# Causal mask of gated linear attention: a triangle multiplied on VectorE as PSUM is read, in place of ScalarE copies and a GpSimd selection

## The chip, the core and the metric

The kernel runs on one core of a Trainium2 chip, in one launch. The metric is device microseconds of that core; the time before is the median of three runs. A profiled execution of its own gives the rows below.

## What is computed

Three stages, one after the other, all in float32:

```python
# 1: gated linear attention, B, H, S, D = 4, 8, 768, 48
f = 1.0 / (1.0 + np.exp(-f_logit))
for t in range(S):
    state = f[:, :, t, :, None] * state + np.einsum('bhd,bhe->bhde', k[:, :, t], v[:, :, t])
    y[:, :, t] = np.einsum('bhd,bhde->bhe', q[:, :, t], state)
# 2: causal softmax attention with E = 4 experts, two chosen for each token; d_model 384, Hd 64
logits = x @ w_gate            # topk, w from these
scores = scale * (x @ wq[e]) @ (x @ wk[e]).T   # causal, softmax -> a
out += mask[..., None] * w[:, :, kk:kk + 1] * (a @ (x @ wv[e]) @ wo[e])
# 3: rotation and mixing over tokens and channels
theta = x @ w_theta
u = x + w_tok_r @ (x * np.cos(theta)) + w_tok_i @ (x * np.sin(theta))
result = u + np.maximum(u @ w_ch, 0.0)
```

## The kernel before

Sequence positions are cut into chunks of 128, so there are six chunks for each of four batches, 24 in all. Within a chunk the gated recurrence becomes dense products. `gate` and `cum` make the running sums of the log gates (a scan on VectorE, line 270) and scale k and q by their exponentials (lines 280 and 281). `att` multiplies k by q for eight heads into two PSUM banks of 128x512 (line 302). Only products of an earlier key with a later query may stay, so `att` then copies each bank to the tile `g_a` on ScalarE (line 90, through `copy`) and clears the other half with a selection on GpSimd (line 309), which cannot start before its copy is done. `out` multiplies the masked `g_a` by v (line 319) and adds what the state carries over (line 325); `state` updates the state (lines 341 to 354). There is one buffer of `g_a`.

`turn_x` splits the result into a rounded part `m_xs`, `m_x` and a remainder for the matmuls of stage 2. There, `val` and `qk` project (lines 477 and 518), and 96 units of one expert and one block of 128 queries go through `score` (558 and 560), `top` (row maxima on VectorE, 566), `exp` (ScalarE, 580), `turn` (transposes 619, copied to `m_aT`), `av` (639), `sum` (651 to 656) and `mix` (668), whose two banks are copied or reduced to `m_xt` and stored.

On the side, 30 blocks of weights that arrive as doubles are turned to float32 with four VectorE operations and one of ScalarE each (lines 107 to 112): three of `w_theta`, and 27 that are stored to a DRAM tile `w_dram` from one staging buffer `w_f`. Stage 3 (`Moe2`, lines 765 to 791) starts when stage 2 is through; its first rotations are made ahead.

All PSUM results share eight banks called `M`. Every piece above is put into one list, `plan`, with a time worked out from the numbers in the table `TUNE`, and the list is walked in order of time. The framework's scheduler then sets each engine's queue, which runs in order. Keys that begin with `e_` say which engine makes a copy, 1 for VectorE and 0 for ScalarE.

Of the kernel before, what the change touches and what calls it, by code (L numbers as in the profile page):

```python
# [7 lines left out]
F32 = mybir.dt.float32  # L8
# [5 lines left out]
OP = mybir.AluOpType  # L14
# [5 lines left out]
P = 128  # L20
# [4 lines left out]
NP = H // 2  # L25
# [30 lines left out]
def make_consts(nc, pool):  # L56
    k = Bag()
    nc.scalar.preload_act_table_set("natural_log_exp_and_others")
    k.ones = pool.tile([P, P], BF16, name="c_ones")
    nc.vector.memset(k.ones, 1.0)  # L60
    k.ident = pool.tile([P, P], F32, name="c_ident")
    ii = k.ident.bitcast(I32)
    nc.gpsimd.iota(ii, pattern=[[1, P]], base=0, channel_multiplier=-1)
    k.one = pool.tile([P, 1], F32, name="c_one")
    nc.vector.memset(k.one, 1.0)
    k.negmask = pool.tile([P, P], BF16, name="c_negmask")
    nc.vector.tensor_scalar(k.negmask, ii, 0.0, NEG, op0=OP.is_gt, op1=OP.mult)
    nc.vector.tensor_scalar(k.ident, ii, 0.0, None, op0=OP.is_equal)
    k.identb = pool.tile([P, P], BF16, name="c_identb")
    nc.vector.tensor_copy(k.identb, k.ident)  # L70
    k.least = pool.tile([P, 2, E, E], F32, name="c_least")
    nc.gpsimd.memset(k.least, TINY)
    nc.gpsimd.affine_select(k.least, k.least, pattern=[[0, 2], [-1, E], [1, E]], base=0, channel_multiplier=0,
                            compare_op=OP.is_ge, fill=0.0)
    k.magic = pool.tile([P, 1], F32, name="c_magic")
    nc.vector.memset(k.magic, MAGIC)
    k.hpi = pool.tile([P, 1], F32, name="c_hpi")
    nc.vector.memset(k.hpi, TWO_PI / 4)
    return k
# [9 lines left out]
def copy(nc, what, out, in_):  # L89
    (nc.vector.tensor_copy if TUNE["e_" + what] else nc.scalar.copy)(out, in_)  # L90
# [141 lines left out]
class Gla:  # L232
# [63 lines left out]
    def att(self, b, c):  # L296
        nc, t = self.nc, self.T[b, c]
        banks = [self.pM.tile([P, NP, P], F32, name="M") for _ in range(2)]
        for hp in range(NP):
            for j, ps in enumerate(banks):  # L300
                r = slice(64 * j, 64 * j + D)
                nc.tensor.matmul(ps[:, hp, :], t.k[r, hp, :], t.q[r, hp, :], start=True, stop=True)  # L302
        yield
        a = self.wk.tile([P, 2, NP, P], F32, name="g_a")
        for j, ps in enumerate(banks):
            copy(nc, f"a{j}", a[:, j], ps)
        yield
        for part in ([a[:, j] for j in range(2)] if b * NT + c < 2 or TUNE['e_mask'] else [a.rearrange("p j n t -> p (j n) t")]):
            nc.gpsimd.affine_select(part, part, pattern=[[0, part.shape[1]], [1, P]], base=0, channel_multiplier=-1,  # L309
                                    compare_op=OP.is_ge, fill=0.0)  # L310
        t.a = a

    def out(self, b, c):
        nc, t = self.nc, self.T[b, c]
# [399 lines left out]
class Moe2:  # L714
# [123 lines left out]


TUNE = dict(  # L840
    y_cum0=0, y_tr0=1.375, y_att0=0.126, y_att1=0.78, y_state0=0, y_turn_x0=0, y_val0=1.729, y_qk0=3.02,
    y_turn0=1.114, y_sum0=0.96, y_sum1=0, y_mix0=1.233, dF1=-0.745, dF2=0.116, dF3=0.979, nw0=44, nw1=9, nw2=10,
    w1=-16.404, w2=-7.547, late_rot=543.893, w_pre=8.523, d_top=0, d_exp=1.229, d_turn=0.792, d_av=0.944,
    d_sum=1.962, alpha=1.291, pre=7.133, l_mix=4.433, mix_sp=14.358, lo0=-10.454, lo_sp=0.19, f0=-21.897,
    f1=-10.255, f2=-0.315, f3=7.902, f4=18.093, f5=44.165, F=46.18, sp=27.869, l_gate=6.566, l_cum=3.387,
    l_tr=7.532, l_att=5.306, l_out=2.063, l_state=2.008, l_xt=0.38, l_val=7.067, v0=7.7, v1=9.035, vsp=5.54,
    l_qk=5.413, qk_sp=0.359, l_q1=10.13, l_top2=2.06, tok0=1.418, tok1=411.066, late0=404.775, late1=504.708,
    late_gap=3.057, ewv=-18.203, ewq=-36.87, esp=3.509, l_factor=4.261, y_factor0=2.51, tok_p=0.109, y_gate0=0.594,
    e_mask=1, e_kn=0, e_a0=0, e_a1=0, e_v=0, e_q=1, e_k=0, e_t0=0, e_t1=0, e_t2=0, e_t3=1, e_yh=0, e_mix0=1,
    e_mix1=0, e_x=0, e_x3=0, e_f=0, y_factor1=0,  # L850
)


# [117 lines left out]
def kernel(ctx: ExitStack, tc: tile.TileContext, arg, out: bass.AP):  # L971
# [10 lines left out]
    rows.tok = (wd[:S], wd[S:2 * S]) if arg.w_tok[0].dtype == I64 else arg.w_tok  # L982
    rows.ch = wd[2 * S:, :DM] if arg.w_ch.dtype == I64 else arg.w_ch
    c = make_consts(nc, const)

    def body(fast):
# [79 lines left out]
```

## Time and profile before

| what | value |
|---|---|
| median of three runs | 647.75 us (647.14 to 649.93) |
| the profiled execution's own time | 653.63 us |
| span of its instructions | 651.7 us |
| mean granted TensorE clock | 0.968 |
| busy: TensorE, VectorE, ScalarE, GpSimd | 604.5, 387.6, 363.6, 131.4 us |

The span runs from the first to the last instruction; the profiled execution's own time has 1.9 us more around it. A busy TensorE is not one at its peak, since the ends of pipelined matmuls are modelled.

### The profile page before, as it was taken

How to read it: one execution, taken by the hardware profiler on the slowest of the kernel's cores; microseconds unless marked ns; L12 is line 12 of the kernel's file. 1: busy time of each engine (PE TensorE's matmuls, PEld its weight loads, DVE VectorE, ACT ScalarE, POOL GpSimd, SP SyncE). 2: the span in 40 equal slices, each digit the busy share in tenths (PEclk: the TensorE clock that was granted, in tenths of full speed). 3: DMA queues.
4: the chain of work that ended last, by engine and by line, in shares of the span. 5: the costliest groups of instructions: out<-in, count | busy, mean ns of one | idle time of the engine just before them, and what ended most of it. 6: DMA issues, size and time to landing. Idle time of an engine off the chain costs nothing.

```text
span 651.7 us, 12652 instructions
## 1 busy us (share of the span) xinstructions
PE 604.5 (93%) x4613; PEld 527.8 (81%) x4613; DVE 387.6 (59%) x932; ACT 363.6 (56%) x919; POOL 131.4 (20%) x205
## 2 busy tenths in 40 slices
PE   5798998999978899999899999988999999999995
PEld 4677767777857778887778878768999999999995
DVE  6788887988888466465566354774775253232221
ACT  6666776765585665666664464876785282130000
POOL 5533211210212012111010010013663141130000
PEclk7699999998999799999899999999899999999999
DMA  7556555665556232324334000616623212000010
GB/s 266 177 173 193 165 182 170 186 191 161 177 187 202 101 98 81 94 83 127 94 96 121 29 32 32 234 57 223 202 78 117 61 49 73 25 24 22 28 49 29
DMA packets 46678, 76.42 MB, mean 117 GB/s; under 512 B 6672, under 2 KB 25616, under 8 KB 46608
## 3 DMA queue, kind: packets, MB, share of 16 engines
q1 hardware_dynamic: 46608, 75.53, 36.6%
q8 instruction: 38, 0.62, 0.4%
q14 instruction: 32, 0.26, 0.1%
HBM read 53.68 MB, written 19.46 MB: 112 GB/s over the span
## 4 chain that ended last, share of the span: by engine, by line
PE 61%; ACT 4%; DMA 4%; DVE 4%; POOL 1%; issue 1%; SPq 1%; ACTq 0%; DVEq 0%; POOLq 0%
PE M L765 22%; PE M L788 6%; PE M L518 5%; PE M L668 5%; PE M L639 4%; PE M L558 4%; PE M L619 3%; PE M L477 3%; PE M L319 2%; PE M L302 2%; PE M L325 2%; DMA g_f<-in_fT_dram 2%; DMA w_dram<-w_f 1%; PE M L777 1%; ACT m_a L580 1%
## 5 line engine op out<-in xcount | busy, mean ns | idle before, releaser
L580 ACT ACTIVATE m_a<-M,m_m 128x384 f32<-128x384 f32 (+4 forms) x128 | 69.2, 548 | 14.3 <-DVE m_m L566 7.1
L566 DVE TENSOR_REDUCE m_m<-M 128x1 f32<-128x384 f32 (+4 forms) x128 | 61.0, 499 | 10.6 <-PE M L560 8.8
L558 PE MATMUL M<-m_ks,m_qs 64*128 64x384 f32 (+4 forms) x256 | 56.0, 482 | 3.1 <-ACT m_aT L90 1.0
L619 PE MATMUL M<-c_ident,m_a 128*128 128x128 f32 x336 | 53.3, 280 | 3.5 <-ACT m_aT L90 1.3
L94 ACT CAST t_uh<-M 128x384 fp32r<-128x384 f32 x24 | 11.3, 474 | 79.3 <-PE M L777 79.3
L309 POOL TENSOR_SCALAR_AFFINE_SELECT g_a<-g_a 128x512 f32<-128x512 f32 x48 | 35.0, 749 | 94.5 <-ACT g_a L90 94.5
L90 ACT COPY m_aT<-M 128x384 f32<-128x384 f32 (+3 forms) x96 | 43.0, 450 | 16.4 <-PE M L619 16.1
L639 PE MATMUL M<-m_aT,m_v 128*64 128x256 f32 (+1 forms) x384 | 43.7, 359 | 0.0
L129 POOL TENSOR_TENSOR t_z0l<-t_ra,t_z0h 128x384 fp32r<-128x384 f32 x23 | 25.0, 1086 | 91.3 <-ACT t_z0h L128 82.9
L619 PEld LDWEIGHTS M<-c_ident,m_a 128*128 128x128 f32 x336 | 38.2, 143 | 5.7 <-ACT m_a L580 2.1
L270 DVE TENSOR_TENSOR_SCAN g_cum<-g_inside,g_f 128x512 f32<-128x512 f32 x24 | 30.6, 1273 | 15.2 <-ACT g_f L266 14.1
L639 PEld LDWEIGHTS M<-m_aT,m_v 128*64 128x64 f32 x384 | 28.7, 137 | 13.0 <-issue 2.1
L319 PE MATMUL M<-g_a,g_v 128*64 128x128 f32 x384 | 30.9, 286 | 7.9 <-POOL g_a L309 7.3
L95 DVE TENSOR_TENSOR t_ul<-M,t_uh 128x384 fp32r<-128x384 f32 x24 | 13.3, 556 | 41.2 <-ACT t_uh L94 41.2
L558 PEld LDWEIGHTS M<-m_ks,m_qs 64*128 64x128 f32 x256 | 24.4, 188 | 16.5 <-issue 4.5
L668 PE MATMUL M<-m_wh,m_yh 128*128 128x384 f32 x96 | 34.1, 357 | 3.7 <-ACT m_aT L90 3.1
L791 DVE SCALAR_TENSOR_TENSOR t_o<-M,t_u 128x384 f32<-128x384 f32 x24 | 13.4, 556 | 39.4 <-PE M L788 39.4
L354 POOL COPY g_block<-g_state 64x192 f32<-64x192 f32 x40 | 18.7, 469 | 86.3 <-DVE g_state L349 73.0
L319 PEld LDWEIGHTS M<-g_a,g_v 128*64 128x64 f32 x384 | 22.9, 140 | 14.1 <-POOL g_a L309 11.2
L302 PE MATMUL M<-g_q,g_k 48*128 48x128 f32 x384 | 32.9, 306 | 1.5 <-DVE g_q L281 0.9
L765 PE MATMUL M<-t_z0h,t_w 128*128 128x384 f32 x96 | 32.8, 342 | 0.0
L668 PE MATMUL M<-m_wh,m_yl 128*128 128x384 f32 x96 | 32.5, 338 | 0.3 <-DVE m_yl L656 0.3
(245 smaller groups left out, 1688.5 us busy)
## 6 DMA issues: line engine op xcount, KB each, us to landing
t_dram<-m_xt SPq DMA_DIRECT2D x24, 384.0 KB, 2.8
g_f<-in_fT_dram SPq DMA_DIRECT2D x24, 256.0 KB, 3.1
g_k<-in_kT_dram SPq DMA_DIRECT2D x24, 256.0 KB, 3.2
g_q<-in_qT_dram SPq DMA_DIRECT2D x24, 256.0 KB, 3.0
g_v<-in_vp_dram SPq DMA_DIRECT2D x24, 256.0 KB, 3.1
w_dram<-w_f SPq DMA_DIRECT2D x27, 192.0 KB, 3.1
w_d<-in_w_tok_r_dram SPq DMA_DIRECT2D x12, 384.0 KB, 3.4
w_d<-in_w_tok_i_dram SPq DMA_DIRECT2D x12, 384.0 KB, 3.9
```

The costliest lines, as they stand in the source:

```text
L90: (nc.vector.tensor_copy if TUNE["e_" + what] else nc.scalar.copy)(out, in_)
L302: nc.tensor.matmul(ps[:, hp, :], t.k[r, hp, :], t.q[r, hp, :], start=True, stop=True)
L309: nc.gpsimd.affine_select(part, part, pattern=[[0, part.shape[1]], [1, P]], base=0, channel_multiplier=-1, compare_op=OP.is_ge, fill=0.0)
L319: nc.tensor.matmul(y[64 * r:64 * r + 64, hp, :], t.v[:, 2 * hp + r, :], t.a[:, r, hp, :], start=hp == 0, stop=c == 0, skip_group_check=True)
L558: nc.tensor.matmul(ps, q[own, rows], k[own, cols], start=True, stop=cols.stop < W)
L566: nc.vector.tensor_reduce(m, ps, axis=AX.X, op=OP.max, negate=True)
L580: self.nc.scalar.activation(a[:, cols], ps, AF.Exp, bias=t.m, accum_out=st.den[:, c, i % 2, e % 2:e % 2 + 1])
L619: nc.tensor.transpose(ps[:, (j - j0) * P:(j - j0 + 1) * P], t.a[:, j * P:(j + 1) * P], self.k.ident)
L639: nc.tensor.matmul(y[64 * r:64 * r + 64, o:TQ], st.v[j][:, m * HD:(m + 1) * HD], st.aT[m][:, j, o:], start=j == 0, stop=True, skip_group_c ...
L668: nc.tensor.matmul(ps[:, :DM], st.y[pr, t // 2][a][:, o], self.wl[c][:, 2 * w0 + pr, :], start=n == 0, stop=n == 5)
L765: nc.tensor.matmul(ps, self.wT[c][h][s][:, (g * G + j) * P:(g * G + j + 1) * P], self.Z[b, s][c][l], start=s == 0 and n == 0, stop=s == NT ...
L788: nc.tensor.matmul(ps[:, :DM], uT[a][:, j, :], self.wl[c][:, j, :], start=n == 0, stop=n == 8)
```

## The change

`att` no longer copies and selects. One VectorE multiply for each bank reads the products out of PSUM, multiplies them by a triangle of ones and zeros (`c_upper`, made once at the start and read again for each of the four head pairs) and writes `g_a`. The second pause inside `att` and its third part go. Four copies change engines by the table: `val`'s `m_v` (`e_v`), the second bank of `mix` for batches 1 to 3 (`e_mix1`) and `turn_x`'s `m_x` (`e_x3`) go from ScalarE to VectorE, `qk`'s `m_qs` (`e_q`) goes from VectorE to ScalarE. `e_a1` and `e_mask` no longer have an effect. Most of the other numbers, which order the pieces, are a little different; TensorE gets 66 warm-up matmuls in place of 63 and otherwise the same matmuls.

```diff
+    k.upper = pool.tile([P, P], F32, name="c_upper")
+    nc.vector.tensor_scalar(k.upper, ii, 0.0, None, op0=OP.is_ge)
...
         yield
-        a = self.wk.tile([P, 2, NP, P], F32, name="g_a")
+        a = t.a = self.wk.tile([P, 2, NP, P], F32, name="g_a")
+        if TUNE["e_fm"]:
+            for j, ps in enumerate(banks):
+                nc.vector.tensor_tensor(a[:, j], ps, self.k.upper.rearrange("p (o t) -> p o t", o=1).to_broadcast([P, NP, P]), op=OP.mult)
+            return
         for j, ps in enumerate(banks):
             copy(nc, f"a{j}", a[:, j], ps)
         yield
         for part in ([a[:, j] for j in range(2)] if b * NT + c < 2 or TUNE['e_mask'] else [a.rearrange("p j n t -> p (j n) t")]):
             nc.gpsimd.affine_select(part, part, pattern=[[0, part.shape[1]], [1, P]], base=0, channel_multiplier=-1,
                                     compare_op=OP.is_ge, fill=0.0)
-        t.a = a
...
-    late_gap=3.057, ewv=-18.203, ewq=-36.87, esp=3.509, l_factor=4.261, y_factor0=2.51, tok_p=0.109, y_gate0=0.594,
-    e_mask=1, e_kn=0, e_a0=0, e_a1=0, e_v=0, e_q=1, e_k=0, e_t0=0, e_t1=0, e_t2=0, e_t3=1, e_yh=0, e_mix0=1,
-    e_mix1=0, e_x=0, e_x3=0, e_f=0, y_factor1=0,
+    ewv=-21.53, ewq=-33.37, esp=3.509, l_factor=4.203, y_factor0=1.518, tok_p=0.558, y_gate0=0.06, e_mask=1, e_fm=1,
+    e_kn=0, e_a0=0, e_a1=1, e_v=1, e_q=0, e_k=0, e_t0=0, e_t1=0, e_t2=0, e_t3=1, e_yh=0, e_mix0=1, e_mix1=1, e_x=0,
+    e_x3=1, e_f=0, y_factor1=0,
```

VectorE's queue at the first chunk, before: the scaled k and q of the second chunk, a remainder of the mixing weights, and what follows.

```order
L280 TENSOR_TENSOR g_k<-g_k,g_ei 128x512
L281 TENSOR_TENSOR g_q<-g_q,g_f 128x512
L95 TENSOR_TENSOR m_wl<-m_a,m_wh 128x384
L187 TENSOR_SCALAR m_ks<-m_ks 128x256
L270 SCALAR_TENSOR_TENSOR g_cum<-g_inside,g_f 128x512
L349 TENSOR_TENSOR g_state<-M,g_dec 128x192
```

The same place now:

```order
L282 TENSOR_TENSOR g_k<-g_k,g_ei 128x512
L283 TENSOR_TENSOR g_q<-g_q,g_f 128x512
L97 TENSOR_TENSOR m_wl<-m_a,m_wh 128x384
L309 TENSOR_TENSOR g_a<-M,c_upper 128x512 x2
L189 TENSOR_SCALAR m_ks<-m_ks 128x256
L354 TENSOR_TENSOR g_state<-M,g_dec 128x192
L272 SCALAR_TENSOR_TENSOR g_cum<-g_inside,g_f 128x512
```

The first chunk's two multiplies stand behind the second chunk's scaling, and the third chunk's scan has moved behind the first state.

VectorE's queue around the sixth gated output `m_ys`, before; `w_d`, `w_b` and `w_f` are the raw, half made and finished weights.

```order
L651 TENSOR_TENSOR m_ys<-M,m_f 128x256
L107 TENSOR_SCALAR w_b<-w_d 128x384
L108 SCALAR_TENSOR_TENSOR w_b<-w_d,w_b 128x384
L656 TENSOR_TENSOR m_yl<-m_ys,m_yh 128x256
L109 SCALAR_TENSOR_TENSOR w_b<-w_d,w_b 128x384
L566 TENSOR_REDUCE m_m<-M 128x1 x2
L112 SCALAR_TENSOR_TENSOR w_f<-w_g,w_b 128x384
```

The same place now:

```order
L656 TENSOR_TENSOR m_ys<-M,m_f 128x256
L661 TENSOR_TENSOR m_yl<-m_ys,m_yh 128x256
L571 TENSOR_REDUCE m_m<-M 128x1 x2
L114 SCALAR_TENSOR_TENSOR w_f<-w_g,w_b 128x384
L109 TENSOR_SCALAR w_b<-w_d 128x384
L110 SCALAR_TENSOR_TENSOR w_b<-w_d,w_b 128x384
L309 TENSOR_TENSOR g_a<-M,c_upper 128x512 x2
L92 COPY m_v<-M 128x260
L111 SCALAR_TENSOR_TENSOR w_b<-w_d,w_b 128x384
```

Two multiplies and a copy of `m_v` now stand inside a weight block's conversion. Over the whole queue, 27 stored blocks stood ahead of the tenth gated output before, and 24 do now; ahead of the first, 4 before and 2 now.

ScalarE's queue between the two exponentials of a pair of units, before:

```order
L580 ACTIVATE m_a,m_den_827<-M,m_m 128x256
L90 COPY g_a<-M 128x512 x2
L90 CAST m_xs<-M 128x3x128
L90 CAST m_x_912<-M 128x128
L580 ACTIVATE m_a,m_den_827<-M,m_m 128x256
```

The same pair now:

```order
L585 ACTIVATE m_a,m_den_822<-M,m_m 128x256
L92 COPY m_aT<-M 128x128
L585 ACTIVATE m_a,m_den_822<-M,m_m 128x256
```

The two copies of `g_a` and the cast of `m_x` are gone from between them, and the cast of `m_xs` stands elsewhere.

## Rows read from the trace of the kernel before

**Rows 1.** Windows by stage: length, busy of each engine (instructions), granted clock, DMA share, GB/s.

```profile
core 0: us, PE busy (x) PEld busy (x) DVE busy (x) ACT busy (x) POOL busy (x), PEclk, DMA share, GB/s
0.00:45.00 45.00, 33.39 (x273) 27.98 (x275) 32.18 (x52) 29.35 (x60) 21.36 (x38) 0.81 0.62 204
45.00:455.00 410.00, 381.19 (x3248) 311.56 (x3249) 278.57 (x748) 264.76 (x715) 65.15 (x125) 0.98 0.42 134
455.00:652.00 197.00, 189.88 (x1095) 188.28 (x1094) 76.89 (x134) 69.54 (x145) 44.91 (x42) 0.99 0.20 63
```

**Rows 2.** Chain that ended last, start of stage 3: start, length, what.

```profile
454.69 15.28 PE M L765 x73
```

**Rows 3.** Waits of PE, 0 to 455 us: total, times, longest.

```profile
PE M L518 <- ACT m_aT L90: 8.9, 4, 3.1
PE M L319 <- POOL g_a L309: 7.3, 10, 2.4
PE M L291 <- DVE g_k L280: 5.9, 2, 4.9
PE M L668 <- ACT m_aT L90: 3.1, 2, 1.6
...
PE M L619 <- ACT m_aT L90: 1.3, 2, 1.1
...
PE M L302 <- DVE g_q L281: 0.9, 1, 0.9
```

**Rows 4.** Timeline of one chunk's mask, 201 us: start, length, what, [idle before].

```profile
200.77 1.05 ACT L90 COPY g_a<-M 128x512 f32<-128x512 f32 x2
...
201.41 1.70 POOL L309 TENSOR_SCALAR_AFFINE_SELECT g_a<-g_a 128x512 f32<-128x512 f32 x2 [5.01 <-ACT g_a L90]
...
202.26 0.43 PE L319 MATMUL M<-g_a,g_v 128*64 128x128 f32 x2 [1.11 <-POOL g_a L309]
...
203.16 1.09 PE L319 MATMUL M<-g_a,g_v 128*64 128x128 f32 x14 [0.47 <-POOL g_a L309]
```

**Rows 5.** Groups of instructions that the change removes or moves.

```profile
L309 POOL TENSOR_SCALAR_AFFINE_SELECT g_a<-g_a 128x512 f32<-128x512 f32 x48 | 35.0, 749 | 94.5 <-ACT g_a L90 94.5
L90 ACT COPY g_a<-M 128x512 f32<-128x512 f32 x48 | 25.8, 597 | 2.9 <-PE M L302 2.3 <-PE M L319 0.6
L90 ACT COPY m_v<-M 128x260 f32<-128x260 f32 x24 | 9.1, 380 | 5.4 <-PE M L477 5.4
L90 ACT COPY m_xt<-M 128x384 f32<-128x384 f32 x18 | 8.7, 482 | 9.4 <-PE M L668 9.4
L90 ACT CAST m_x<-M 128x128 fp32r<-128x128 f32 x24 | 6.9, 287 | 0.0
L90 DVE COPY m_qs<-M 128x256 f32<-128x256 f32 x24 | 10.0, 418 | 3.3 <-PE M L518 3.3
```

**Rows 6.** Groups of instructions nearest to those that it adds.

```profile
L566 DVE TENSOR_REDUCE m_m<-M 128x1 f32<-128x512 f32 x16 | 10.2, 678 | 0.0
L280 DVE TENSOR_TENSOR g_k<-g_k,g_ei 128x512 f32<-128x512 f32 x24 | 17.4, 723 | 12.2 <-DMA g_k<-in_kT_dram 11.4 <-ACT g_ei L276 0.7
L90 DVE COPY m_xt<-M 128x384 f32<-128x384 f32 x24 | 13.2, 550 | 3.2 <-PE M L668 3.2
L456 DVE TENSOR_TENSOR m_x<-M,m_x 128x128 fp32r<-128x128 f32 x24 | 6.7, 281 | 0.0
L90 ACT COPY m_ks<-M 128x256 f32<-128x256 f32 x24 | 9.2, 381 | 8.0 <-PE M L518 7.9
```

**Rows 7.** Windows, 60 to 220 and 220 to 455 us; columns as in Rows 1.

```profile
60.00:220.00 160.00, 143.53 (x1251) 116.44 (x1251) 129.76 (x335) 106.07 (x283) 29.71 (x56) 0.98 0.57 176
220.00:455.00 235.00, 224.46 (x1850) 184.15 (x1851) 135.42 (x375) 149.36 (x406) 30.22 (x62) 0.97 0.31 99
```

**Rows 8.** Window 60 to 220 us, GpSimd's selections of line 309 alone.

```profile
60.00:220.00 160.00, 14.68 (x20) 0.98 0.57 176
```

**Rows 9.** Waits of VectorE, 60 to 220 us: total, times, longest.

```profile
DVE w_f L112 <- DMA w_dram<-w_f: 13.2, 9, 3.0
```

More of the change, by code (lines that the diff above doesn't have):

```diff
@@ L840 @@
 TUNE = dict(
[L841 to L847, printed above, removed]
-    late_gap=3.057, ewv=-18.203, ewq=-36.87, esp=3.509, l_factor=4.261, y_factor0=2.51, tok_p=0.109, y_gate0=0.594,
-    e_mask=1, e_kn=0, e_a0=0, e_a1=0, e_v=0, e_q=1, e_k=0, e_t0=0, e_t1=0, e_t2=0, e_t3=1, e_yh=0, e_mix0=1,
-    e_mix1=0, e_x=0, e_x3=0, e_f=0, y_factor1=0,
+    y_cum0=0, y_tr0=1.335, y_att0=0, y_att1=0.736, y_state0=0, y_turn_x0=0.062, y_val0=1.476, y_qk0=3.025,
+    y_turn0=1.154, y_sum0=0.89, y_sum1=0.251, y_mix0=1.233, dF1=-0.596, dF2=0.511, dF3=-0.746, nw0=43, nw1=13,
+    nw2=10, w1=-19.838, w2=-7.547, late_rot=530.633, w_pre=8.753, d_top=0.022, d_exp=1.342, d_turn=0.792,
+    d_av=0.907, d_sum=1.962, alpha=1.291, pre=7.669, l_mix=4.71, mix_sp=14.358, lo0=-6.586, lo_sp=0.618, f0=-20.969,
+    f1=-10.431, f2=-0.209, f3=7.693, f4=15.999, f5=44.165, F=47.57, sp=27.869, l_gate=7.678, l_cum=3.64, l_tr=6.33,
+    l_att=5.068, l_out=1.832, l_state=1.211, l_xt=0.073, l_val=7.067, v0=6.561, v1=9.035, vsp=5.54, l_qk=5.413,
+    qk_sp=1.899, l_q1=11.411, l_top2=2.125, tok0=2.039, tok1=417.747, late0=398.706, late1=497.921, late_gap=3.737,
+    ewv=-21.53, ewq=-33.37, esp=3.509, l_factor=4.203, y_factor0=1.518, tok_p=0.558, y_gate0=0.06, e_mask=1, e_fm=1,
+    e_kn=0, e_a0=0, e_a1=1, e_v=1, e_q=0, e_k=0, e_t0=0, e_t1=0, e_t2=0, e_t3=1, e_yh=0, e_mix0=1, e_mix1=1, e_x=0,
+    e_x3=1, e_f=0, y_factor1=0,
 )
```

## The prediction

> **What bounds the kernel now.** I first cut the span into stages [rows 1]. From 455 us on the kernel is in stage 3, where TensorE is busy 189.9 us of some 197 and VectorE and ScalarE less than 40% each. The chain that ended last runs through TensorE from the first matmul of that stage, 73 of them in 15.28 us without a break [rows 2]. The change leaves those matmuls and their feeders as they are, so these 197 us stay, and whatever the change is worth has to come out of the first 455 us.
>
> There, TensorE is busy 33.4 of the first 45 us and 381.2 of the next 410 (93%). The list of what it waited for [rows 3] says which idle time is whose. The three largest entries that end on ScalarE's copies of `m_aT` are 8.9, 3.1 and 1.3 us, 13.3 together; what these wait for is a PSUM bank that ScalarE has not yet emptied. The entry that ends on GpSimd's selection is 7.3 us in ten waits. The 5.9 us on `g_k` belong to the start, where the first inputs and weights arrive. VectorE appears after the start only in small entries, the largest being 0.9 us for `g_q`.
>
> So TensorE is close to the bound and idles a little behind ScalarE and GpSimd. The reader should see next where VectorE stands: between 60 and 220 us, where the weight blocks are converted, it is busy 129.8 of 160 us (81%), while ScalarE is at 106.1 (66%); between 220 and 455 us it is at 135.4 of 235 (58%) [rows 7]. Of VectorE's 30.2 idle us in the first of these stretches, 13.2 are waits for the one staging buffer `w_f` to be stored [rows 9].
>
> **What goes.** GpSimd loses 48 selections, 35.0 us busy, and ScalarE 48 copies, 25.8 us busy [rows 5]. One mask shows the path that is cut [rows 4]: the copies begin at 200.77, the first selection at 201.41, and TensorE's `out` begins at 202.26 behind the first and goes on at 203.16 behind the second. It takes 1.49 us to the first half and 2.39 to the second.
>
> **What comes.** No row of before has a multiply of 128x512 that reads PSUM. From below, ScalarE's copy of that size takes 597 ns [rows 5]; from above, VectorE's product of two 128x512 tiles takes 723 [rows 6]. Nearest is VectorE's maximum over 128x512 read from the same PSUM, 678 ns, and I take that: 48 x 0.678 = 32.5 us (28.7 to 34.7). With 0.68 for the first half and 1.36 for both, TensorE can start a mask's first half about 0.8 us and its second about 1.0 us sooner, if VectorE begins when ScalarE did.
>
> **What moves.** VectorE takes 24 casts of `m_x` at 0.281 (6.7 us), 18 copies of `m_xt` at 0.550 (9.9) and 24 copies of `m_v`, priced like its own copy of 128x256, 0.418 (10.0); it gives up the 10.0 us of `m_qs` [rows 5, 6]. The sum for VectorE is 32.5 + 6.7 + 9.9 + 10.0 - 10.0 = 49.1 us more. ScalarE loses 25.8 + 9.1 + 8.7 + 6.9 and takes `m_qs` at the 0.381 of `m_ks` (9.2): 41.3 us less. Almost all of it lies in the first 455 us, so over the 410 us stretch VectorE goes from 68% to about 79% and ScalarE from 65% to about 55%.
>
> **What that is on the path.** Three terms, against the median of 647.75 us. The profiled execution took 653.63, 1.9 of it around its span, and is 5.9 us above that median; I apply the differences to the median.
>
> First, the ten waits for the selection, 7.3 us. They average 0.73, about what the shorter path saves, but the longest is 2.4 and can only be shortened. I take 5 us of gain (bounds 0 and 7.3).
>
> Second, the 13.3 us behind ScalarE. Its queue loses 41.3 of some 294 us, 14%; by that share alone 1.9 us would go. But copies of `g_a` and casts of `m_x` that stood directly ahead of exponentials and `m_aT` copies are gone from between them, so more than the share should go. I take 5 us (bounds 0 and 13.3).
>
> Third, what VectorE now does late. In the stretch of 60 to 220 us there are 20 selections, so ten chunks [rows 8]; each brings 2 x 0.678 + 0.281 + 0.418 - 0.418 = 1.64 us more, 16.4 for ten. VectorE then is at 146 of 160 us, 91%, less some 2 us for the conversions that the new order puts later. Its queue is in order: a multiply that waits for its matmuls, or for `out` to release the one buffer of `g_a`, holds up the row maxima behind it, and ScalarE's exponentials wait for those. On ScalarE the same two waits cost 2.9 us in all (2.3 and 0.6) [rows 5]. I take 4 us of loss (bounds 0 and 16.4, if no idle time of VectorE can be used).
>
> The small ones: `c_upper` is one operation of 128x128, 0.28 us by the nearest row of that shape [rows 6], at the start; at worst it lengthens the 5.9 us wait there by as much. Three more warm-up matmuls lie beside TensorE's 11.6 idle us of the first 45 [rows 1]. GpSimd was busy 65.2 of 410 us and has less to do now, so nothing new waits for it. The copies that change engine free the same banks a little later on VectorE (0.418 for 0.380, 0.550 for 0.482), which is in the third term. The remaining numbers of the table shift pieces by a few us; I give them no sign of their own. Sum: 647.75 - 5 - 5 + 4 = 641.75, so **642 us**.
>
> **Rivals.** *VectorE becomes the bound and it is slower.* The place is 60 to 220 us. If its waits there (the 13.2 us for the store of `w_f`, which the change leaves, and the rest of the 30.2) stay where they are, the 16.4 us of new work lengthen the stretch in full, while the 7.3 us behind GpSimd go: 647.75 + 16.4 - 7.3 = 656.9, **657 us**. It decides from the point where VectorE is over about 95% busy in that stretch, 152 of 160 us. For it speaks that VectorE already is the busiest engine after TensorE and that two multiplies now stand inside a conversion; against it, that most of its work (the conversions) has no one waiting, and that TensorE waits for it hardly at all now.
> The Trainium skill speaks for this rival: "Perfetto Trace Analysis", section "Optimizing Scalar/DVE Operations", says that when VectorE is saturated it may pay to hand work to ScalarE or even GpSimd, and the change hands it the other way. The trace agrees that VectorE is the fuller of the two (81% against 66%), not that it is saturated; by that rule the time would come out on the side of 657, not of 642.
>
> *Nothing to measure.* TensorE is at 93% through this part and its matmuls don't change. The waits could merely change names: what no longer waits for a selection waits for VectorE's multiply, and the bank that ScalarE frees sooner is freed later by VectorE. The second term is then 0 and the first and third, 5 and 4, cancel: 647.75 - 5 + 4 = 646.75, **647 us**.
>
> *More than forecast.* Both reliefs come in full and VectorE's extra work fits in its idle time: 647.75 - 7.3 - 13.3 = 627.15, **627 us**. For it speaks that most of VectorE's work has slack; against it that waits rarely vanish on a path with TensorE at 93%.
>
> **Chances.** The forecast (633 to 644.5 us) 0.42, more than forecast 0.10, nothing to measure 0.23, VectorE as the bound 0.25. The three runs of before lie within 0.43% of each other, so 0.5% (3.2 us) is about what can be told from no change; faster by more 0.52, within it 0.23, slower 0.25. The range is 630 to 657: below it lies the better half of the good rival, above it the worse part of the bad one, together not over 2 in 10. Since cases of both signs hold most of the chance, the forecast's own range is 633 to 644.5.
>
> **What would show it.** Right: the multiply's row at 0.65 to 0.72 us with 48 of them; no entry for GpSimd before line 324, and an entry for VectorE's `g_a` there under 3 us; TensorE's entries for ScalarE's `m_aT` under 9 us; stage 3 as long as now, its first matmul about 6 us sooner. VectorE at 88 to 94% while the weights are converted. Wrong: TensorE's waits for `g_a`, or ScalarE's for the row maxima, grow by more than the 10 us that the two gains give; or VectorE's row for the multiply is well above 0.72; or the start, the first 45 us [rows 1], comes out several us longer by the new order alone.

## The result, and the profile after

The changed kernel took 641.3 us (median of four runs, 639.34 to 643.9) against 648.36 for the kernel before in the same session: a ratio of 0.9892 [0.9847, 0.9938]. A later repeat gave 640.91 us and 0.9901 [0.9868, 0.9933]. So the change is faster by some 7 us, and 642 was forecast. In the experiments below a median is that of all runs of a kernel, while a ratio leaves out the slow ones (one or two in three of the kernels), so where the two differ the ratio counts.

The page of the changed kernel's profiled execution (642.42 us) begins so:

```profile
span 640.6 us, 12539 instructions
## 1 busy us (share of the span) xinstructions
PE 595.1 (93%) x4616; PEld 517.7 (81%) x4616; DVE 420.2 (66%) x1023; ACT 327.9 (51%) x829; POOL 93.1 (15%) x157
```

Its windows, with the columns of [rows 1]; the second ends at 445 us, since stage 3 starts sooner:

```profile
0.00:45.00 45.00, 33.26 (x288) 27.45 (x288) 31.53 (x58) 25.26 (x49) 16.48 (x32) 0.81 0.64 199
45.00:445.00 400.00, 374.83 (x3242) 305.23 (x3241) 311.44 (x834) 233.28 (x636) 31.67 (x83) 0.98 0.43 137
60.00:220.00 160.00, 144.99 (x1281) 118.18 (x1281) 141.28 (x370) 98.62 (x264) 12.83 (x38) 0.97 0.54 172
```

VectorE is at 141.28 of 160 us (88%) where the weights are converted, against 81% in [rows 7], and ScalarE at 62%. TensorE's share is what it was. What TensorE waited for up to 445 us, as in [rows 3]:

```profile
PE M L523 <- ACT m_aT L92: 7.6, 4, 3.8
PE M L293 <- DVE g_k L282: 6.6, 2, 5.6
PE M L563 <- ACT m_ks L92: 3.9, 3, 2.7
PE M L673 <- ACT m_a L585: 2.3, 2, 1.9
PE M L523 <- DMA m_xs<-m_x: 2.2, 1, 2.2
PE M L324 <- DVE g_a L309: 1.8, 2, 1.6
PE M L346 <- ACT m_a L585: 1.5, 1, 1.5
PE M L624 <- ACT m_a L585: 1.3, 2, 1.1
```

The entry for GpSimd is gone, and VectorE's `g_a` stands in its place with 1.8 us in two waits. Behind ScalarE there are now entries for `m_ks` and `m_a` that [rows 3] did not have at that size. The groups that were added, by form, with the columns of [rows 5]:

```profile
L309 DVE TENSOR_TENSOR g_a<-M,c_upper 128x512 f32<-128x512 f32 x48 | 31.0, 683 | 3.0 <-PE M L304 2.7 <-PE M L324 0.2
...
L92 DVE COPY m_v<-M 128x260 f32<-128x260 f32 x24 | 10.1, 421 | 11.0 <-PE M L482 10.8
L92 DVE CAST m_x<-M 128x128 fp32r<-128x128 f32 x24 | 6.9, 286 | 9.7 <-ACT m_xs L92 9.4
```

A multiply takes 683 ns, and VectorE stood idle before them for 3.0 us in all. The timeline of one mask shows the shorter path that answers to [rows 4]:

```profile
193.21 1.28 DVE L309 TENSOR_TENSOR g_a<-M,c_upper 128x512 f32<-128x512 f32 x2
194.58 0.85 PEld L324 LDWEIGHTS M<-g_a,g_v 128*64 128x64 f32 x16 [0.17 <-issue]
194.58 1.09 PE L324 MATMUL M<-g_a,g_v 128*64 128x128 f32 x16
```

All sixteen products run without a break, beginning 1.37 us after the multiplies began; before, the second half started 2.39 us after the copies. VectorE's waits between 60 and 220 us, and ScalarE's up to 445:

```profile
DVE w_f L114 <- DMA w_dram<-w_f: 0.9, 2, 0.7
```

```profile
ACT m_a L585 <- DVE m_m L571: 21.5, 14, 3.5
...
ACT m_a L585 <- DVE m_m L574: 16.0, 10, 4.4
```

The 13.2 us behind the store of `w_f` [rows 9] are nearly gone. ScalarE's exponentials wait 21.5 + 16.0 = 37.5 us for VectorE's row maxima, in the profile of before 13.7:

```profile
ACT m_a L580 <- DVE m_m L566: 7.1, 8, 1.2
ACT m_a L580 <- DVE m_m L569: 6.6, 11, 1.2
```

The profiled execution of before is 6 us above its median, so a difference of the two profiles holds too much. One of the experiments below, `before_side_new`, keeps TensorE's queue of before and was profiled at 647.65 us, which is the median of 25 runs of before beside it. I use it as the stand-in for before. What its TensorE waited for behind `m_aT` and the selection, in the two largest entries:

```profile
PE M L518 <- ACT m_aT L90: 8.5, 4, 2.6
PE M L319 <- POOL g_a L309: 8.2, 11, 2.4
```

Its row and that of the changed kernel, each from the start to the 37th matmul of stage 3:

```profile
0.00:444.70 444.70, 406.57 (x3497) 332.47 (x3498) 306.08 (x794) 288.77 (x764) 81.76 (x161) 0.97 0.44 139
```

```profile
0.00:437.90 437.90, 402.69 (x3501) 328.05 (x3502) 338.97 (x887) 253.53 (x676) 45.12 (x113) 0.96 0.45 142
```

The stretch is 6.8 us shorter. Of that, TensorE's idle time gives 38.13 - 35.21 = 2.9 us, and its busy time 406.57 - 402.69 = 3.9, with three more warm-up matmuls and one more of the late ones. That the busy time fell was in no term of the prediction, and the granted clock did not do it: it is 0.97 in the stand-in's row and 0.96 in the other. The scores alone (lines 558 and 563, 256 matmuls in both), in windows from 0 to 445 us of the stand-in and of the changed kernel:

```profile
0.00:445.00 445.00, 54.86 (x256) 0.97 0.44 139
```

```profile
0.00:445.00 445.00, 50.12 (x256) 0.97 0.45 144
```

The same 256 matmuls keep TensorE busy 4.7 us less. Two timelines show how, the stand-in first (the same piece stands at 366.75 us in the profile of before):

```profile
363.39 0.65 PE L639 MATMUL M<-m_aT,m_v 128*64 128x256 f32 x2
363.97 0.70 PE L558 MATMUL M<-m_ks,m_qs 64*128 64x256 f32 x2
364.60 0.86 PE L639 MATMUL M<-m_aT,m_v 128*64 128x256 f32 x6
365.39 0.70 PE L558 MATMUL M<-m_ks,m_qs 64*128 64x256 f32 x2
```

And the changed kernel:

```profile
355.28 0.38 PE L624 MATMUL M<-c_ident,m_a 128*128 128x128 f32 x2
355.59 0.70 PE L563 MATMUL M<-m_ks,m_qs 64*128 64x256 f32 x4
```

A pair of units has the scores of two experts, each a product over 64 rows that the profile shows as two matmuls. Where the two experts' products stand next to each other, all four matmuls are through in 0.70 us, so the products run side by side. Where something stands between them, two take 0.70 us and the other two 0.70 again. In the records of the whole span, 19 of the stand-in's 256 score matmuls overlap other score matmuls for less than half their length, 9.1 us of them, and 2 in the changed kernel. No list of waits shows this, since an unpaired matmul counts as busy.

### The profile page after: what moved, and what is told of

Its sections match the earlier page's. It is cut to its first block, busy times and chain, and to the rows that moved or that the text cites. A ratio compares the mean times of both kernels' runs of the same rounds, so it can differ in the third digit from the quotient of the medians.

```text
span 640.6 us, 12539 instructions
## 1 busy us (share of the span) xinstructions
PE 595.1 (93%) x4616; PEld 517.7 (81%) x4616; DVE 420.2 (66%) x1023; ACT 327.9 (51%) x829; POOL 93.1 (15%) x157
## 5 line engine op out<-in xcount | busy, mean ns | idle before, releaser
L585 ACT ACTIVATE m_a<-M,m_m 128x384 f32<-128x384 f32 (+4 forms) x128 | 68.9, 545 | 41.0 <-DVE m_m L571 21.5
L563 PE MATMUL M<-m_ks,m_qs 64*128 64x384 f32 (+4 forms) x256 | 50.1, 478 | 4.6 <-ACT m_ks L92 3.9
L92 ACT COPY m_aT<-M 128x384 f32<-128x384 f32 (+3 forms) x96 | 42.0, 448 | 20.4 <-PE M L624 20.1
L96 ACT CAST t_uh<-M 128x384 fp32r<-128x384 f32 x24 | 11.3, 476 | 77.8 <-PE M L782 77.8
L272 DVE TENSOR_TENSOR_SCAN g_cum<-g_inside,g_f 128x512 f32<-128x512 f32 x24 | 29.8, 1242 | 15.9 <-ACT g_f L268 15.8
L644 PEld LDWEIGHTS M<-m_aT,m_v 128*64 128x64 f32 x384 | 26.4, 140 | 15.4 <-ACT m_aT L92 1.6
L563 PEld LDWEIGHTS M<-m_ks,m_qs 64*128 64x128 f32 x256 | 22.7, 187 | 13.8 <-ACT m_ks L92 5.0
L309 DVE TENSOR_TENSOR g_a<-M,c_upper 128x512 f32<-128x512 f32 x48 | 31.0, 683 | 3.0 <-PE M L304 2.7
L770 PE MATMUL M<-t_z0h,t_w 128*128 128x384 f32 x96 | 32.8, 342 | 0.0
L523 PE MATMUL M<-m_xs,w_qh 128*128 128x256 f32 x144 | 23.8, 299 | 9.4 <-ACT m_aT L92 7.2
L770 PE MATMUL M<-t_z1h,t_w 128*128 128x384 f32 x96 | 32.3, 336 | 0.2 <-DVE t_w L97 0.2
```

Source lines behind the costliest of these rows:

```text
L272: nc.vector.tensor_tensor_scan(flat(t.cum), flat(self.inside), flat(t.f), initial=0.0, op0=OP.min, op1=OP.add)
L309: nc.vector.tensor_tensor(a[:, j], ps, self.k.upper.rearrange("p (o t) -> p o t", o=1).to_broadcast([P, NP, P]), op=OP.mult)
L563: nc.tensor.matmul(ps, q[own, rows], k[own, cols], start=True, stop=cols.stop < W)
L585: self.nc.scalar.activation(a[:, cols], ps, AF.Exp, bias=t.m, accum_out=st.den[:, c, i % 2, e % 2:e % 2 + 1])
L644: nc.tensor.matmul(y[64 * r:64 * r + 64, o:TQ], st.v[j][:, m * HD:(m + 1) * HD], st.aT[m][:, j, o:], start=j == 0, stop=True, skip_group_c ...
L770: nc.tensor.matmul(ps, self.wT[c][h][s][:, (g * G + j) * P:(g * G + j + 1) * P], self.Z[b, s][c][l], start=s == 0 and n == 0, stop=s == NT ...
```

## The experiments

Eleven kernels ran, and the changed kernel once more, as given above. The ratios are to runs of before on the same chip.

**The parts alone.** First the multiply by itself: the changed code with the table of before.

```diff
+    e_fm=1   # all other numbers and engines of copies as before
```

> The kernel before with the multiply by the triangle alone: its order numbers and its engines for the four copies are kept. Theory 1 (the gain is that of the mask's shorter path and of ScalarE's lost copies): 641 to 645 us. Rival A (the gain is that of the new order numbers): 646 to 652. Rival B (the gain needs the copies on the engines where they are now): 646 to 650.

It took 653.08 us, ratio 1.0073 [1.0046, 1.0099]: slower, above all three ranges, and against the theory that the multiply carries the gain. Its waits of TensorE up to 445 us:

```profile
PE M L293 <- DVE g_k L282: 7.4, 3, 5.6
PE M L523 <- ACT m_aT L92: 7.2, 4, 2.8
...
PE M L713 <- DVE m_aT L114: 2.8, 3, 1.9
PE M L304 <- DVE g_a L309: 2.4, 2, 1.4
...
PE M L324 <- DVE g_a L309: 2.1, 2, 1.6
```

GpSimd's entry (8.2 us in the stand-in) is gone, but the entries that name VectorE add to 18.9 us in place of 12.1, and all entries before stage 3 to 37.6 in place of 37.7. The waits only changed their name. The loss lies in TensorE's busy time, 411.43 us up to the 37th matmul of stage 3 against 406.57 in the stand-in:

```profile
0.00:449.40 449.40, 411.43 (x3498) 336.36 (x3499) 328.93 (x843) 266.56 (x718) 45.12 (x113) 0.95 0.43 138
```

The granted clock of that stretch is 0.95 against 0.97. By the first `mix` this run is 5.2 us behind (94.7 against 89.5), and from 45 to 95 us its clock was 0.90, against 0.97. Whether a lower clock comes with the edit stays open, since of its nine runs the one with the highest mean clock (0.980) took 652.92 us.

Then the other numbers alone, with copies and selection as before:

```diff
-    e_fm=1, e_a1=1, e_v=1, e_q=0, e_mix1=1, e_x3=1   # the changed kernel's other numbers stay
+    e_fm=0, e_a1=0, e_v=0, e_q=1, e_mix1=0, e_x3=0
```

> The changed kernel's order numbers alone: mask by ScalarE copies and GpSimd selection, and the four copies on the engines of before. Theory 1: 646 to 651 us, as before or a little worse, since these numbers were made for another mask. Rival A: 640 to 644.

It took 656.6 us, ratio 1.0121 [1.0077, 1.0166], above both ranges; the profiled execution took 664.04, so only its rows of waits and busy time are read. The scores and the waits for the selection:

```profile
0.00:445.00 445.00, 51.45 (x256) 0.96 0.42 136
PE M L324 <- POOL g_a L315: 10.8, 14, 2.4
```

The scores take nearly as little as in the changed kernel, but TensorE waits for the selection 10.8 us, 7.6 of them in the first 95, where the stand-in has 3.1. The new order pairs the scores, and with copy and selection TensorE waits longer for the mask than in the old one.

Next the changed kernel with its four copies back on their old engines:

```diff
-    e_v=1, e_q=0, e_mix1=1, e_x3=1
+    e_v=0, e_q=1, e_mix1=0, e_x3=0
```

> The changed kernel with m_v, the second bank of mix and m_x back on ScalarE and m_qs back on VectorE. VectorE has 16.6 us less, ScalarE 15.5 more. Theory 1: 638 to 644 us, no clear difference to the change. Rival B: 645 to 650.

646.23 us, ratio 0.9959 [0.9933, 0.9984], as rival B had it: more than half of the gain is gone without them, though the scores stay at 50.1 us. And the converse, multiply and copies on their new engines, all other numbers of before:

```diff
+    e_fm=1, e_v=1, e_q=0, e_mix1=1, e_x3=1   # other numbers as before
```

> The multiply and the four copies on their new engines, with the order numbers of before. Theory 2 (mask, copies and numbers fit each other; the numbers say where in each in-order queue a piece stands): 649 to 655 us, about as slow as the multiply alone with those numbers (653). Rival B (the copies' engines are what the multiply needs): 641 to 646.

651.31 us, ratio 1.0074 [1.0041, 1.0108], as theory 2 had it. The scores take as long as in the stand-in, and VectorE's entries in TensorE's waits add to 20.8:

```profile
0.00:445.00 445.00, 54.86 (x256) 0.97 0.44 139
```

With the old numbers, the whole change of operations gains nothing.

**The path through two engines.** In the changed kernel, VectorE copies each bank and GpSimd selects, so VectorE's load stays nearly the same (a copy takes 683 ns, like the multiply); the second pause of `att` is back too:

```diff
-    e_fm=1, e_a0=0
+    e_fm=0, e_a0=1   # e_a1=1 stays
```

> The changed kernel, but VectorE only copies each bank and GpSimd selects as before. VectorE's and ScalarE's loads are those of the change; only GpSimd's stage is back in the path, 0.64 us for the first half and 1.3 for both. If the shorter path is worth the 5 us of the forecast's first term: 645 to 648 us. If the relief of ScalarE is nearly all of it: 640 to 643.

652.0 us, ratio 1.0059 [1.0030, 1.0087], some 11 us above the changed kernel and above both ranges. TensorE's waits in the first 95 us:

```profile
PE M L324 <- POOL g_a L315: 8.0, 9, 2.4
PE M L293 <- DVE g_k L282: 6.9, 2, 6.0
```

Over the first 452 us that entry is 11.1 us in 14 waits (profiled at 656.37 us, above the median); the first score comes at 48.8 us, against 43.5 in the changed kernel. The other second stage, on ScalarE:

```diff
-                nc.vector.tensor_tensor(a[:, j], ps, self.k.upper..., op=OP.mult)
+                nc.scalar.copy(a[:, j], ps)
+                nc.vector.tensor_tensor(a[:, j], a[:, j], self.k.upper..., op=OP.mult)
```

> The changed kernel, but ScalarE copies each bank to g_a first and VectorE multiplies g_a in place: ScalarE has its 48 copies back (26 to 29 us), VectorE's load is nearly the same, GpSimd stays out. If the relief of ScalarE is the larger part of the gain: 647 to 652 us. If the stage that is gone from the path is (the VectorE copy with GpSimd selection cost 652): the path has again two steps, 0.6 and 0.7 us, and it comes to 648 to 654 by that alone; TensorE's waits for g_a tell the two apart, over 8 us for the path and under 4 for ScalarE's load.

652.58 us, ratio 1.0078 [1.0051, 1.0104]. Its first waits of TensorE up to 442 us:

```profile
PE M L325 <- DVE g_a L310: 9.0, 11, 2.5
PE M L293 <- DVE g_k L282: 7.1, 4, 5.2
PE M L524 <- ACT m_aT L92: 5.3, 2, 3.2
```

The mask again ends TensorE's waits (9.0 us, 6.3 of them in the first 95), while `m_aT` waits are fewer than in the changed kernel, though ScalarE has 26.0 us more to do. All entries before stage 3 add to 37.7 us, 3.0 more than in the changed kernel; TensorE's busy time there is 4.4 us longer (407.1 against 402.7; profiled at 649.53 us). So a second engine in the path costs, whichever it is, and ScalarE's load does not show. Waits for the mask are not the whole of the 11 us, though: in both runs the framework's scheduler also moved a few groups of matmuls in TensorE's queue, in its first 95 us.

**VectorE's room.** Each multiply made twice into the same tile, 48 x 0.683 = 32.8 us more:

```diff
-            for j, ps in enumerate(banks):
-                nc.vector.tensor_tensor(a[:, j], ps, ...)
+            for j, ps in enumerate(banks * 2):
+                nc.vector.tensor_tensor(a[:, j % 2], ps, ...)
```

> The changed kernel with each multiply made twice, the same values written again: 48 more operations of 0.68 us on VectorE, 32.8 us. If VectorE is nearly the bound while weights are converted: 655 us or more, 0.68 to 1 us for most of the 24 chunks and the stretch of 60 to 220 us longer by over 8 us. If VectorE's queue still has slack: 643 to 648 us, since only the 1.4 us longer path of each mask shows where TensorE waits for it.

658.81 us, ratio 1.0179 [1.0137, 1.0221]: 18 us above the changed kernel. The time is that of the first theory, the place is not:

```profile
60.00:220.00 160.00, 148.59 (x1291) 119.69 (x1290) 139.13 (x358) 92.26 (x248) 13.54 (x38) 0.96 0.49 151
```

VectorE is no fuller there than in the changed kernel (141.28). The first score is 6.6 us late (50.1 against 43.5 us), the 103rd 8.7 (215.2 against 206.5), so some 2 us of the loss lie in the stretch in which over 8 were expected; by the 180th it is 15.6 (337.3 against 321.7). The mask is also ready later by two multiplies and holds its banks longer, so this run prices load and delay together, and it doesn't tell how near VectorE's limit is. TensorE's waits for `g_a` at line 324 are 4.4 us. By the rule that the prediction cited from the Trainium skill, "Perfetto Trace Analysis", section "Optimizing Scalar/DVE Operations", it may make sense to take work off a saturated VectorE. The time went the way of that rule, but the trace does not show its condition, with VectorE at 87% of that stretch against 88% in the changed kernel.

**Which of the numbers.** The last four split the 52 other numbers, always against the whole set. First the seven that place the conversions and the late stage, set back, with TensorE's queue unchanged:

```diff
-    tok_p=0.558, tok0=2.039, tok1=417.747, late0=398.706, late1=497.921, late_gap=3.737, late_rot=530.633
+    tok_p=0.109, tok0=1.418, tok1=411.066, late0=404.775, late1=504.708, late_gap=3.057, late_rot=543.893
```

> After's kernel with the seven numbers that place the weight conversions, and the late ones of stage 3, set back to those of before; TensorE's queue stays as it is. If the conversions' spread is the part of the new numbers that the change needs: 647 us or more (ratio above 1.0 to 0.997), and VectorE's waits for the store of w_f come back, over 8 us in place of 0.9. If it is the order of the matmul pieces: 640 to 643 us (ratio 0.988 to 0.993) whatever w_f waits. If every departure from the fitted numbers costs alike: 644 to 647 us, as for the other two groups.

640.91 us, ratio 0.987 [0.9824, 0.9916]: nothing is lost, and the waits for the store of `w_f` stay at 0.9 us. The theory of the conversions' spread falls, for the time and for the waits. The same seven in before, the new values in place of the old:

```diff
-    tok_p=0.109, tok0=1.418, ...   # in the kernel before
+    tok_p=0.558, tok0=2.039, ...
```

> Before's kernel with only the seven numbers of the conversions taken from after; TensorE's queue stays as in before. If the spread of the conversions is a gain by itself that the change happened to bring along: 641 to 645 us (ratio 0.990 to 0.995), with waits for the store of w_f under 3 us in place of 14. If it only makes room for the multiplies: 646 to 651 us (ratio 0.997 to 1.005).

647.82 us, ratio 0.9997 [0.9969, 1.0024], with 11.3 us of waits for the store up to 445 us, where before had 14.2. These numbers are worth nothing, with the change or without it. Then the numbers of the start, the loads and the chunks' spacing:

```diff
-    f0=-20.969, lo0=-6.586, dF3=-0.746, nw1=13, ewv=-21.53, ...   # 19 numbers
+    f0=-21.897, lo0=-10.454, dF3=0.979, nw1=9, ewv=-18.203, ...
```

> After's kernel with the nineteen numbers of the start, the first loads and the chunks' spacing set back. If the needed part of the new numbers is the start: 646 us or more, with the first score at 45 us or later (43.5 in after, 45.5 in before) and the loss there by 100 us. If it is the conversions or the lags within a chunk: 640 to 643 us. If every departure costs alike: 644 to 647 us.

648.38 us, ratio 1.0025 [0.9995, 1.0056]: 7 us above the changed kernel. The profiled execution (643.65) was the fastest of ten and had the highest mean clock (0.979, the others 0.961 to 0.972), so its trace cannot be held against the median. In it the first score is at 44.6 us, sooner than that theory asked, but TensorE's waits behind VectorE add to 20.4 us up to stage 3, against 12.3 in the changed kernel; the largest:

```profile
PE M L324 <- DVE g_a L309: 6.9, 3, 3.7
PE M L293 <- DVE g_k L282: 6.4, 2, 6.1
```

Last the lags within a chunk and a unit:

```diff
-    y_qk0=3.025, y_sum1=0.251, l_gate=7.678, l_tr=6.33, l_state=1.211, qk_sp=1.899, l_q1=11.411, ...   # 26 numbers
+    y_qk0=3.02, y_sum1=0, l_gate=6.566, l_tr=7.532, l_state=2.008, qk_sp=0.359, l_q1=10.13, ...
```

> After's kernel with the twenty-six lags within a chunk and within a unit (when a piece follows the one before, and what it yields to) set back. The multiply makes g_a ready sooner than copy and selection did, so if the lags are what fits the change: 646 us or more, and TensorE's waits for g_a or for m_aT grow by 5 us or more over after's 1.8 and 8.7. If not: 640 to 643 us. If every departure costs alike: 644 to 647 us.

648.99 us, ratio 0.9989 [0.9960, 1.0019]: by the ratios some 6 us above, so neither of these two groups can go back alone. Its scores, from 0 to 445 us (profiled at 654.6 us, above its median):

```profile
0.00:445.00 445.00, 58.92 (x256) 0.95 0.43 137
```

They keep TensorE busy 8.8 us longer than in the changed kernel, with 32 of 256 unpaired (ten of the 256 ran at least in part at half clock, four in the changed kernel). So the lags carry the pairing, and the named waits say little of it: they add to 37.1 us, against 34.7, and those for `g_a` and `m_aT` did not grow by the 5 us expected (3.0 and 10.9, against 1.8 and 9.7).

## Why the prediction was right in its total, and what of it was wrong

*The multiply and VectorE's load.* 0.678 was taken and 0.683 measured; 91% was expected between 60 and 220 us and 88% came. The sums of load were too large: VectorE's busy time rose by 32.6 us (387.6 to 420.2), not by 49.1, and ScalarE's fell by 35.7 (363.6 to 327.9), not by 41.3. The sum for VectorE added durations, but those of neighbours overlap (48 multiplies of 683 ns make 31.0 us of busy time), and other operations became shorter, as that at line 282 (below). `c_upper` took 0.566 us, not 0.28.

*Waits behind GpSimd, 5 us of gain.* The entry fell from 8.2 in the stand-in to nothing, and VectorE's entries, 1.8 us for `g_a` among them, add to what they did before (below). In place of 5 us the whole entry went, 3.2 more. But this is right only within the new order. In `mask_only` the same entry went, and others grew by as much: there the rival of waits that change their names was the true one, and the time even rose. In the new order the second stage costs more than it did before, 11.1 us of waits in `dve_copy_select`.

*Waits behind ScalarE, 5 us of gain.* This step failed, with the largest error of all, 8.0 us. The entries for `m_aT` did fall, from 13.4 us in the stand-in to 9.7, but those for `m_ks`, `m_a` and others came up, and all of ScalarE's entries before stage 3 rose from 17.2 to 20.2. Its share of work was not what made ScalarE late: its exponentials wait for VectorE's maxima 37.5 us, where they waited 13.7 us in the profile of before. `act_copy_dve_mult`, with the load given back, had 15.8 us behind ScalarE, less than the changed kernel.

*VectorE late, 4 us of loss.* It was expected that the row maxima would be held up, and they were. TensorE did not feel it at VectorE's own entries (12.1 and 12.3 us); the 3.0 us more behind ScalarE is where it would show.

*The numbers, no sign.* This step failed too. Of the 6.8 us gained up to stage 3, 4.7 are the pairing of scores, in TensorE's busy time, and it comes with the lags of the table: `order_only` has it without the multiply, `old_numbers` lacks it with the multiply. Undoing the start costs some 7 us, undoing the lags some 6. Up to stage 3 the account is 3.0 us of named waits (8.2 off GpSimd, 3.0 on ScalarE, 2.0 on a DMA, 0.2 on VectorE), 4.7 of scores, less 0.9 for everything else: 6.8 us. The profile of the later repeat agrees, with 34.4 us of named waits and 50.59 of scores. The forecast had 6 from its three terms alone (5, 5 and -4), which came as 8.2, -3.0 and -0.2. The total agreed by luck: the errors of the terms nearly cancelled.

*The store of `w_f`.* The text held that its 13.2 us would stay; 0.9 stayed. `side_old` and `before_side_new` show that the numbers for the conversions did not do it, and `mask_only`, with 3.6 us in that stretch, that the multiplies by themselves shorten it:

```profile
DVE w_f L114 <- DMA w_dram<-w_f: 3.6, 5, 1.8
```

Presumably VectorE comes to the next store later. The rival at 657 counted this idle time as unusable, and it was used.

*VectorE as the bound.* It did not decide: 88% is short of the 95% that the text asked for, a level that no run here tests. In `twice` most of the loss lies outside that stretch.

*The signs.* Of those of being right, the entry for `m_aT` missed (9.7 us, asked were under 9). One of being wrong came true: ScalarE's waits for the row maxima grew by 23.8 us (13.7 to 37.5), over the 10 that were named, and the kernel was faster all the same. It was a poor sign, since it counts idle time of ScalarE; all that TensorE waits behind ScalarE grew by 3.0.

Stage 3 began 6.8 us sooner, as the text said (about 6). It was not quite as long as before: from its 37th matmul to the end the changed kernel takes 202.7 us, the stand-in 201.0 and the profile of before 204.0, so between the two profiles 5.1 of the 6.8 us are left.

Two explanations stay argued and not shown. One is that the numbers fit the multiply in particular: `start_old` and `inner_old` lose as much as some kernels whose operations were changed, so part of the 11 us of `dve_copy_select` may be no more than an order that suits it less. Its 11.1 us of named waits speak against that being all. The other is why TensorE is busy 4.9 us longer in `mask_only`.

## What to carry to other kernels

Where queues run in order, an edit and the order that goes with it are one change: here each alone was slower by 0.7 to 1.2%, and both together faster by 1.1%. Read TensorE's busy time by line before and after, not its waits alone: matmuls over half the rows that lose their partner count as work. A term for "this engine has less to do" needs a row that shows the engine late for want of time, not one that merely names it as the releaser.

## What the runs showed of the hardware

Two score matmuls over 64 rows each, in opposite halves of the rows, ran side by side: four of 64x256 in 0.70 us, the same time as two of one half. VectorE's copy of 128x512 out of PSUM and its product of the same bank with a triangle both took 683 ns, so here the mask costs nothing beyond the copy; read from its own tile, the product took 696. VectorE's product of two tiles at line 282 fell from 723 ns [rows 6] to 699, though nothing in it was changed. GpSimd's selections alone are not the reason: with them back it is at 703 (`dve_copy_select`) and 706 (`order_only`); the cause stays open. The rows of the copy and of the product read from its own tile:

```profile
L92 DVE COPY g_a<-M 128x512 f32<-128x512 f32 x48 | 30.8, 683 | 3.9 <-PE M L304 3.5 <-PE M L324 0.5
L310 DVE TENSOR_TENSOR g_a<-g_a,c_upper 128x512 f32<-128x512 f32 x48 | 31.5, 696 | 11.0 <-ACT g_a L309 10.9
```
